# One single expert slot moved from behind eight double slots to in front of them

## The chip, the core and the metric

The kernel runs on one core of one Trainium2 chip. The time is that of the device for one execution, in microseconds (us); the median of three runs counts. The profile is of one further execution, which has a time of its own.

## What is computed

Three layers follow one another. The first is an attention over 4 batches, 8 heads and 576 positions, which keeps only scores within `tau` of the maximum. The second is a layer of eight experts. Each of the 2304 tokens goes to one of them:

```python
for s in range(S):
    fresh_e = int(np.argmax(logits[b, s]))
    e = fresh_e if s == 0 or local_gate[b, s] < 0.5 else (prev_e if prev_e >= 0 else fresh_e)
    prev_e = e
    ...
    h = np.maximum(x[b, s] @ w1[e], 0.0)      # w1[e]: 512 x 1024
    out[b, s] = p[e] * (h @ w2[e])            # w2[e]: 1024 x 512
```

The third mixes tokens and channels: `theta = x @ w_theta`, then `u = x + w_tok_r @ (x cos theta) + w_tok_i @ (x sin theta)`, and `u + relu(u @ w_ch)`. Everything is in float32.

## The kernel before

The experts work in **slots**. A single slot is 128 tokens of one expert, a double slot (a "two") is 256 tokens of one expert. Three early single slots are settled when three of the four batches are routed; they run first, in the order 2, 1, 0, while the last batch is being routed. Then come the late slots, found by `late_slots` from the final counts: eight twos (`NTWOS`), one single (`NSINGLE`), and two single slots called final (`NFINAL`), which hold no token of the first batch. In all there are 14 slots in `self.states`; below they go by their place, 0 to 13. Before, places 3 to 10 are the twos, 11 is the single and 12 and 13 are the finals.

`late_slots` writes a small table, `order_tab`, of three rows: where in the list of tokens a slot begins, its expert, and whether that expert differs from the one of the slot before. SyncE reads the table (`load_index` L911, `load_w1`). The third entry is the condition of the eight loads of 512 KB with which a slot gets its expert's weights, 4.19 MB: four of `w1` into `w1r` and three parts of `raw` (L961), four of `w2` into four `w2r` (L973). Where it is 0 the loads are issued and move nothing, and the slot uses what lies in the buffers.

A load is split into a high and a low part, by ScalarE and VectorE (`split`, L1096 and L1097); of `w1` and `w2` a single slot splits three quarters and a two splits all. The buffer `xt` for a slot's token rows has one copy. GpSimd gathers the rows into it (`gather`, L924) with the indices that SyncE has loaded (`load_index`, L916), and TensorE transposes them out of it (`tokens`, L938).

`slot_step` runs place `i`. It issues the gather of the next slot first. For a single slot (`single_step`) TensorE then does, in this order: `hidden` of this slot (L1023 to L1029), `tokens` of the next, `finish_slot` of the last if that was single (L1062 to L1066), `hidden_out` of this slot (L1049). SyncE's `load_index` for the slot after the next comes behind the load of this slot's fourth part of `w2`, and that waits until `finish_slot` of the last slot has read the buffer with L1066. For a two (`two_step`) TensorE does the four parts of `hidden_two` (L994 to L996), with `finish_slot` of the last slot among them if that was single, then `tokens` of the next, then `finish_two` (L1011 to L1013). Steps that decode the weights of the third layer (`decode`; GpSimd's share is L1168 and L1176) stand in the twos. Results go to DRAM by `scatter` (L1085) once ScalarE has scaled them (L1079).

TensorE, ScalarE and VectorE keep the order that is written out by hand in a step; the order on SyncE and GpSimd is a planner's. After place 13, all engines pass a branch on the number of left-over slots (L761), and the third layer begins with L1366.

Of the kernel before, what the change touches and what calls it, by code (L numbers as in the profile page):

```python
# [31 lines left out]
NEARLY, NTWOS, NSINGLE, NFINAL, MAXSINGLE = 3, 8, 1, 2, 8  # L32
# [20 lines left out]
class Kernel:  # L53
# [574 lines left out]
    def late_slots(self):  # L628

        nc = self.nc  # L630
        cnt = self.counts()
        yield
        used = self.early["used"]
        ni = self.small("late_ni", [1, E], I32)
        nc.vector.scalar_tensor_tensor(ni, used[:, :E], float(-P), cnt, ALU.mult, ALU.add)
        nc.vector.tensor_scalar(ni, ni, float(P - 1), None, ALU.add)
        nc.vector.tensor_scalar(ni, ni, 7, None, ALU.logical_shift_right)
        nf = self.small("late_nf", [1, E])
        nc.vector.tensor_copy(nf, ni)
        yield  # L640


        odd = self.small("late_odd", [1, E], I32)
        nc.vector.tensor_scalar(odd, ni, 1, None, ALU.bitwise_and)
        key = self.small("late_key", [1, E])
        nc.vector.scalar_tensor_tensor(key, odd, 16.0, self.slotj[:, 1:1 + E], ALU.mult, ALU.add)
        has = self.small("late_has", [1, E])
        nc.vector.tensor_tensor(has, nf, self.slots0, ALU.is_gt)
        nc.vector.tensor_tensor(key, key, has, ALU.mult)
        top = self.small("late_top", [1, 2])  # L650
        nc.vector.tensor_reduce(top[:, 0:1], key, AX.X, ALU.max)
        rest = self.small("late_rest", [1, E])
        nc.vector.scalar_tensor_tensor(rest, key, top[:, 0:1], key, ALU.is_lt, ALU.mult)
        nc.vector.tensor_reduce(top[:, 1:2], rest, AX.X, ALU.max)
        fin = self.small("late_fin", [1, E])
        nc.vector.scalar_tensor_tensor(fin, key, top[:, 1:2], has, ALU.is_ge, ALU.mult)
        nc.vector.tensor_tensor(nf, nf, fin, ALU.subtract)
        fbase = self.small("fin_base", [1, E + 1])
        nc.vector.memset(fbase, 0.0)
        nc.vector.tensor_tensor(fbase[:, :E], used[:, :E], nf, ALU.add)  # L660
        nc.vector.tensor_copy(ni, nf)
        final = yield from self.slot_table("final", NFINAL, 1, fin, fbase)
        yield
        nc.vector.tensor_scalar(ni, ni, 1, None, ALU.logical_shift_right)
        ntwo = self.small("late_two", [1, E])
        nc.vector.tensor_copy(ntwo, ni)
        twos = yield from self.slot_table("twos", NTWOS, 2, ntwo, used)
        yield
        two = twos["used"]
        nc.vector.scalar_tensor_tensor(nf, two[:, :E], -2.0, nf, ALU.mult, ALU.add)  # L670
        base = self.small("late_base", [1, E + 1])
        nc.vector.scalar_tensor_tensor(base, two, 2.0, used, ALU.mult, ALU.add)
        single = yield from self.slot_table("single", MAXSINGLE, 1, nf, base)

        yield
        n, m = NTWOS + NFINAL + MAXSINGLE, NTWOS + NSINGLE
        tab = self.small("order_tab", [1, 3, n])
        nc.vector.tensor_copy(tab[:, :2, :NTWOS], twos["tab"])
        nc.vector.tensor_copy(tab[:, :2, NTWOS:m], single["tab"][:, :, :NSINGLE])
        nc.vector.tensor_copy(tab[:, :2, m:m + NFINAL], final["tab"])  # L680
        nc.vector.tensor_copy(tab[:, :2, m + NFINAL:], single["tab"][:, :, NSINGLE:])
        e = tab[:, 1]
        nc.vector.tensor_tensor(tab[:, 2, 0:1], e[:, 0:1], self.early["tab"][:, 1, 0:1], ALU.not_equal)
        nc.vector.tensor_tensor(tab[:, 2, 1:], e[:, 1:], e[:, :n - 1], ALU.not_equal)
        tabi = self.cpool.tile([1, 3, n], I32, name="order_tabi")
        nc.vector.tensor_copy(tabi, tab)
        self.late = dict(tabi=tabi, total=single["total"])
# [45 lines left out]
    def first_loads(self):  # L733

        self.w1raw = [self.w1r] + [self.raw[:, i * F:(i + 1) * F] for i in range(3)]
        slots = [("early", j, False) for j in reversed(range(NEARLY))]
        slots += [("late", j, j < NTWOS) for j in range(NTWOS + NSINGLE + NFINAL)]
        self.states = [
            dict(slot=s[:2], two=s[2], first=i == 0, final=i >= len(slots) - NFINAL, extra=False) for i, s in enumerate(slots)]
        self.load_index(self.states[0])  # L740
        self.load_w1(self.states[0], 0)
        for st in self.states[1:NEARLY]:
            self.load_index(st)
# [825 lines left out]
```

## Time and profile before

| what | value |
|---|---|
| three runs | 858.43, 859.72 and 860.22 us, median 859.72 us |
| the profiled execution | 859.51 us, of which the profile's span is 857.8 us |
| TensorE busy | 814.5 us, 95% of the span |
| VectorE, ScalarE, GpSimd busy | 614.5, 494.2 and 211.9 us |
| read from and written to DRAM | 98.67 and 16.58 MB |

The attention takes about the first 303 us, the experts follow to 603.39 us, where the third layer begins. A row of the timeline has the start in us from the span's start, the duration in us, the engine, the line, the operation, what it writes and reads, and a count; a bracket gives the time for which the engine sat idle before it and what ended that. Matmuls overlap their neighbours, so a piece of work is measured from the start of its first instruction to the start of what follows.

### The profile page before, as it was taken

Reading aid. Unit: us, or ns where it says so; the run is one execution under the profiler, and the core shown is the slowest. Engines: PE = TensorE matmul, PEld = TensorE weight load, DVE = VectorE, ACT = ScalarE, POOL = GpSimd, SP = SyncE. Lnnn points to the kernel's source line nnn. Section 1 sums busy time; section 2 is a strip of 40 time slices with the busy share of each in tenths; the row PEclk is TensorE's granted clock in tenths of the full one; section 3 lists DMA queues with packets and bytes.
Section 4 is the critical chain, followed back from the end, with each engine's and each line's share of the span. In section 5 each row is a group of like instructions: output and inputs, shape, how many; then the busy total and the mean of one; then the engine's idle time right before and its main releaser. Section 6 shows DMA issues by size and latency. Waiting matters only on the chain. (4 is left out here: it accounts for less than half of the span.)

```text
span 857.8 us, 15181 instructions
## 1 busy us (share of the span) xinstructions
PE 814.5 (95%) x5554; PEld 655.2 (76%) x5554; DVE 614.5 (72%) x1281; ACT 494.2 (58%) x883; POOL 211.9 (25%) x209
## 2 busy tenths in 40 slices
PE   7999999999999898899999999989788999999997
PEld 4555655656566555789999899856778999999997
DVE  6888788888979849859888987544498845755432
ACT  5888777877777745656555555545654445535311
POOL 3000002002003014426555544101153520332120
PEclk9999999999999999999999999999898999999999
DMA  6622213322431369278777787666012030030101
GB/s 167 156 63 75 85 58 94 89 58 70 114 90 38 98 228 230 62 239 303 269 273 257 235 286 233 235 209 190 17 50 72 16 105 1 2 105 1 56 1 56
DMA packets 67241, 106.88 MB, mean 125 GB/s; under 512 B 28370, under 2 KB 34902, under 8 KB 67160
## 3 DMA queue, kind: packets, MB, share of 16 engines
q1 hardware_dynamic: 62968, 95.33, 36.3%
q0 software_dynamic: 4192, 10.51, 3.6%
q8 instruction: 46, 0.75, 0.4%
q14 instruction: 35, 0.29, 0.1%
HBM read 98.67 MB, written 16.58 MB: 134 GB/s over the span
## 5 line engine op out<-in xcount | busy, mean ns | idle before, releaser
L315 ACT ACTIVATE e<-ns,nb 128x576 f32<-128x576 f32 x144 | 112.1, 779 | 43.5 <-DVE ns L309 41.5
L309 DVE TENSOR_SCALAR_CACHE_REDUCE ns<-s,nqs 128x576 f32<-128x576 f32 x144 | 116.8, 812 | 25.4 <-PE s L289 14.3
L347 DVE SCALAR_TENSOR_TENSOR a<-ns,thr,e 128x576 f32<-128x576 f32 x144 | 117.2, 814 | 1.7 <-ACT thr L322 1.3
L289 PE MATMUL s<-raw 64*128 64x288 f32 x512 | 87.3, 440 | 7.7 <-DVE ns L309 7.1
L362 ACT ACTIVATE aT<-t 128x512 f32<-128x512 f32 x128 | 70.4, 594 | 21.7 <-PE t L361 20.8
L402 PE MATMUL o<-aT,vm 128*64 128x288 f32 x512 | 76.3, 418 | 0.0
L994 PE MATMUL h<-xh,stk 128*128 128x256 f32 x256 | 73.2, 286 | 0.0
L995 PE MATMUL h<-xl,stk 128*128 128x256 f32 x256 | 72.5, 283 | 0.0
L996 PE MATMUL h<-xh,stk 128*128 128x256 f32 x256 | 72.4, 283 | 0.0
L361 PE MATMUL t<-ident,a 128*128 128x128 f32 x512 | 69.6, 276 | 1.5 <-ACT aT L362 1.5
L1097 DVE TENSOR_TENSOR w2l<-w2r,w2h 128x1024 fp32r<-128x1024 f32 x50 | 64.8, 1311 | 7.5 <-ACT w2h L1096 7.4
L289 PEld LDWEIGHTS s<-raw 64*128 64x128 f32 x512 | 42.0, 185 | 36.1 <-DVE ns L309 17.0
L361 PEld LDWEIGHTS t<-ident,a 128*128 128x128 f32 x512 | 57.0, 141 | 14.2 <-issue 10.1
L402 PEld LDWEIGHTS o<-aT,vm 128*64 128x64 f32 x512 | 31.5, 136 | 37.0 <-issue 23.8
L1096 ACT ACTIVATE w2h<-w2r 128x1024 fp32r<-128x1024 f32 x50 | 52.2, 1061 | 10.4 <-DMA w2r<-in_moe_w_dram 7.9
L1011 PE MATMUL o<-w2h,hh 128*128 128x512 f32 x128 | 50.6, 395 | 0.0
L1012 PE MATMUL o<-w2l,hh 128*128 128x512 f32 x128 | 50.1, 391 | 0.4 <-DVE w2l L1097 0.4
L1013 PE MATMUL o<-w2h,hl 128*128 128x512 f32 x128 | 50.0, 390 | 0.0
L994 PEld LDWEIGHTS h<-xh,stk 128*128 128x128 f32 x256 | 49.1, 192 | 0.8 <-DVE hl L999 0.3
L995 PEld LDWEIGHTS h<-xl,stk 128*128 128x128 f32 x256 | 49.1, 192 | 0.5 <-issue 0.2
L996 PEld LDWEIGHTS h<-xh,stk 128*128 128x128 f32 x256 | 49.1, 192 | 0.0
L1097 DVE TENSOR_TENSOR stk<-raw,stk 128x1024 fp32r<-128x1024 f32 x36 | 43.9, 1241 | 7.2 <-ACT stk L1096 7.0
(382 smaller groups left out, 2160.0 us busy)
## 6 DMA issues: line engine op xcount, KB each, us to landing
w2r<-in_moe_w_dram SPq DMA_DIRECT2D x56, 512.0 KB
raw<-in_moe_w_dram SPq DMA_DIRECT2D x42, 512.0 KB
raw<-in_q_dram SPq DMA_DIRECT2D x15, 576.0 KB
w1r<-in_moe_w_dram SPq DMA_DIRECT2D x14, 512.0 KB
raw<-in_k_dram SPq DMA_DIRECT2D x30, 176.0 KB
vm<-in_v_dram SPq DMA_DIRECT2D x32, 128.0 KB
scr_x<-x SPq DMA_DIRECT2D x16, 256.0 KB
out_dram<-ob SPq DMA_DIRECT2D x16, 256.0 KB
```

Source lines behind the costliest of these rows:

```text
L289: nc.tensor.matmul(s[:, z, :SH], qd[rows, int(j != z), cs], kd[rows, j * KH:j * KH + SH], start=True, stop=True)
L309: nc.vector.tensor_scalar(ns, s[:, :, :SH], self.nqs[:, 0:1], None, ALU.mult, ALU.min, accum_out=nb)
L315: self.nc.scalar.activation(e, pr["s", c, j], AF.Exp, bias=pr["nb", c][:, j:j + 1], scale=-1.0)
L347: nc.vector.scalar_tensor_tensor(a.rearrange("p (z s) -> p z s", z=2), s, thr, e, ALU.is_le, ALU.mult, accum_out=total)
L361: nc.tensor.transpose(t[:, i, :], al(c)[:, k * P:(k + 1) * P], self.ident)
L362: nc.scalar.activation(aT[:, 4 * j:4 * j + 4, c * P:(c + 1) * P], t, AF.Copy)
L402: nc.tensor.matmul(o[j * D:(j + 1) * D, :SH], vm[:, j, c - 1, :], aT[:, 4 * j + c - 1, zs], start=(z == 0 and c == 1), stop=(z == 1 and c ...
L994: nc.tensor.matmul(h[:, i], wh[:, fs], xh, start=(k == 0), stop=False)
L995: nc.tensor.matmul(h[:, i], wh[:, fs], xl, start=False, stop=False)
L996: nc.tensor.matmul(h[:, i], wl[:, fs], xh, start=False, stop=(k == 3))
L1096: nc.scalar.activation(hi, raw, AF.Copy)
L1097: nc.vector.tensor_tensor(lo, raw, hi.bitcast(F32), ALU.subtract)
```

## The change

In `order_tab` and in the list of slots the single slot comes in front of the twos. It has place 3 now, the twos have 4 to 11, and the finals stay at 12 and 13. The two copies into `order_tab` write other columns; the row that tells whether the expert differs is worked out from the new order by the same instructions.

```diff
-        nc.vector.tensor_copy(tab[:, :2, :NTWOS], twos["tab"])
-        nc.vector.tensor_copy(tab[:, :2, NTWOS:m], single["tab"][:, :, :NSINGLE])
+        nc.vector.tensor_copy(tab[:, :2, NSINGLE:m], twos["tab"])
+        nc.vector.tensor_copy(tab[:, :2, :NSINGLE], single["tab"][:, :, :NSINGLE])
...
-        slots += [("late", j, j < NTWOS) for j in range(NTWOS + NSINGLE + NFINAL)]
+        slots += [("late", j, NSINGLE <= j < NTWOS + NSINGLE) for j in range(NTWOS + NSINGLE + NFINAL)]
```

## Rows read from the trace of the kernel before

**Rows 1.** Stretches: us, busy per engine (instructions), granted TensorE clock, DMA share, GB/s.

```profile
303.00:360.70 57.70, 51.07 (x243) 35.17 (x243) 46.16 (x137) 30.98 (x48) 20.77 (x14) 0.94 0.66 176
360.70:553.20 192.50, 192.13 (x1234) 174.46 (x1233) 149.20 (x165) 105.96 (x143) 87.41 (x56) 1.00 0.76 253
553.20:603.40 50.20, 42.10 (x166) 28.73 (x164) 21.91 (x24) 25.12 (x38) 5.99 (x6) 0.97 0.58 195
```

**Rows 2.** Timeline of TensorE, behind the twos, places 11 to 13.

```profile
553.21 0.39 PE L1023 MATMUL h<-stk,xh 128*128 128x512 f32 x1
...
559.00 0.60 PE L938 MATMUL t<-ident,xt 128*128 128x128 f32 x4
...
560.86 0.50 PE L1023 MATMUL h<-stk,xh 128*128 128x512 f32 x1 [0.82 <-ACT xh L941]
...
570.37 1.09 PE L938 MATMUL t<-ident,xt 128*128 128x128 f32 x4 [2.58 <-DMA xt<-scr_x,idx]
571.11 0.78 PE L1062 MATMUL o<-w2h,hh 128*128 128x512 f32 x1
...
578.13 0.60 PE L1049 MATMUL t<-ident,h 128*128 128x128 f32 x4
579.50 0.50 PE L1023 MATMUL h<-stk,xh 128*128 128x512 f32 x1 [0.77 <-ACT xh L941]
...
585.84 0.79 PE L1062 MATMUL o<-w2h,hh 128*128 128x512 f32 x1
...
592.08 1.04 PE L1049 MATMUL t<-ident,h 128*128 128x128 f32 x8
593.56 0.50 PE L1062 MATMUL o<-w2h,hh 128*128 128x512 f32 x1 [0.44 <-ACT hh L1050]
...
598.76 1.96 PE L1066 MATMUL o<-w2r,hf 128*128 128x512 f32 x4 [0.55 <-DMA w2r<-in_moe_w_dram]
603.39 0.74 PE L1366 MATMUL v<-ident,raw 128*128 128x128 f32 x5 [2.68 <-PEq L761]
```

**Rows 3.** Stretches, columns as in rows 1: ten us behind the longest stall.

```profile
570.00:580.00 10.00, 8.86 (x32) 6.39 (x32) 3.84 (x4) 4.97 (x8) 0.00 (x0) 0.83 0.62 228
```

**Rows 4.** Timelines of GpSimd, SyncE and ScalarE in the same stretch.

```profile
542.72 0.99 POOL L924 DMA_INDIRECT xt<-scr_x,idx  x1 [10.25 <-PE t L938]
...
563.74 1.43 POOL L924 DMA_INDIRECT xt<-scr_x,idx  x1 [8.39 <-PE h L1025]
...
563.21 2.64 SPq L973 DMA_DIRECT2D w2r<-in_moe_w_dram  x3
...
600.97 0.69 ACT L1079 ACTIVATE raw<-o,idx 128x512 f32<-128x512 f32 x1 [6.91 <-DMA scr_m<-raw,idx]
```

**Rows 5.** Timeline of TensorE ahead of the first two.

```profile
353.28 0.63 PE L938 MATMUL t<-ident,xt 128*128 128x128 f32 x4 [0.42 <-DMA xt<-scr_x,idx]
353.67 0.48 PE L1062 MATMUL o<-w2h,hh 128*128 128x512 f32 x1
...
359.71 1.04 PE L1049 MATMUL t<-ident,h 128*128 128x128 f32 x8
```

**Rows 6.** Stretches, columns as in rows 1, and SyncE's timeline ahead of the first two.

```profile
350.00:360.00 10.00, 9.57 (x42) 6.54 (x41) 8.62 (x11) 8.85 (x12) 1.48 (x2) 1.00 0.24 75
...
350.85 1.67 SPq L961 DMA_DIRECT2D raw<-in_moe_w_dram  x3
359.78 0.07 SPq L973 DMA_DIRECT2D w2r<-in_moe_w_dram  x1
360.38 0.38 SPq L916 DMA_DIRECT2D idx<-scr_list  x1
```

**Rows 7.** Timeline of GpSimd ahead of the first two.

```profile
341.79 5.42 POOL L1176 TENSOR_TENSOR th<-w 128x512 fp32r<-128x512 f32 x3 [10.30 <-DMA w2r<-in_moe_w_dram]
...
349.48 0.96 POOL L924 DMA_INDIRECT xt<-scr_x,idx  x1 [0.30 <-issue]
...
362.96 0.98 POOL L924 DMA_INDIRECT xt<-scr_x,idx  x1 [11.18 <-DMA idx<-scr_list]
```

## The prediction

> **What bounds the kernel now.** I read the stretches first. From 360.70 to 553.20 us, the eight twos, TensorE is busy for 192.13 of 192.50 us at the full granted clock [rows 1]: nothing but matmul work counts there, and 253 GB/s of transfers lie hidden beside it. In the stretches on either side, where single slots run, it is busy for 51.07 of 57.70 and 42.10 of 50.20 us, at granted 0.94 and 0.97. So the change is worth what it does to waits in these two stretches, since every matmul, split, gather and scatter is still made. Next I read TensorE's timeline there, for the bracketed waits [rows 2, 5], and then the queues that they name [rows 4, 6, 7].
>
> The end goes thus [rows 2]. Place 11 begins at 553.21, its hidden layer lasts until the transposes of place 12's tokens at 559.00, and place 12's hidden layer begins at 560.86 after a wait of 0.82. Then TensorE waits 2.58 for the gathered tokens of place 13 and transposes them at 570.37. That gather could only be issued at 563.74, since the one buffer was read at 559.00 by place 12, and three weight loads went out at about the same time, from 563.21 on [rows 4]. After the wait the clock falls: granted 0.83 in 570 to 580, a mix of 2.4 and 1.2 GHz [rows 3]. Further waits of 0.77, 0.44 and 0.55 follow, then the branch.
>
> **Which loads the change removes.** I worked the experts of the slots out of the reference's routing with its inputs. The final counts of the eight experts are 521, 178, 345, 351, 172, 172, 227 and 338. After three batches 354, 123, 254, 274, 138, 152, 182 and 251 are there, so the early slots have experts 0, 0 and 2 and run as 2, 0, 0. What is left is 3, 2, 2, 3, 2, 2, 2 and 3 slots; the finals take one of 3 and one of 7, the twos are of 0 to 7, the single is of 0. Before, the order is 2, 0, 0, then 0 to 7, 0, 3, 7; after, 2, 0, 0, 0, then 0 to 7, 3, 7. Twelve slots fetched weights, eleven will: 4.19 MB less. The trace bears out how a skipped load looks: three loads of 512 KB for place 3 are issued from 350.85 on, 1.57 MB in all, but the ten us from 350 to 360 moved only 75 GB/s, 0.75 MB in sum [rows 6]; the repeated 0 was skipped.
>
> Do the bytes themselves cost time? The end moved 195 GB/s and the twos 253 without a wait [rows 1], so the end was held by the order of its steps more than by the rate. I take nothing for bytes. The Trainium skill (DMA: Bandwidth & Descriptors, section Specifications) puts the limit from memory at about 358 GB/s for a core; by it 195 is no ceiling, and fewer bytes in the end gain nothing by themselves. Were 195 the ceiling, the 4.19 MB would be 21.5 us instead of the 19.2 below, and the sum 852.1.
>
> **The end, after.** With the single gone, two slots follow the last two. Place 12 now stands where 11 stood: its tokens were transposed within the last two, so the buffer is free early and the gather for 13 goes out as that at 542.72 did, some 16 us ahead of its use [rows 4]. The path of TensorE, from rows 2: hidden layer of 12, tokens of 13 and the wait of 0.82, which stays, 553.21 to 560.86, 7.65. Hidden layer of 13, 579.50 to 585.84, 6.34. Finish of 12, 585.84 to 592.08, 6.24. Transposes of 13 with the wait of 0.44, to 593.56, 1.48. Finish of 13 up to L1066, 5.20 less the wait of 0.55, since its last load has no third slot's weights ahead of it, 4.65. From L1066 to the third layer, 4.63. Sum 31.0 against 603.39 - 553.21 = 50.2: **19.2 us less**. What is late next is w2 of place 13: its loads go out at 563.21 as those of 12 did, and the finish needs it at about 575. ScalarE's wait of 6.91 for the scatter before the last scaling [rows 4] ends at 600.97, just behind TensorE; it may give back up to 0.6, which I leave out.
>
> **The head, after.** Place 3 is a single in front of the first two. It adds to TensorE one hidden layer, 559.00 - 553.21 = 5.79 [rows 2]; one finish, 359.71 - 353.67 = 6.04, and its transposes, 1.04 [rows 5]; and one set of token transposes, about 0.5. Sum 13.4. The wait of 0.42 for the second half of the first two's tokens [rows 5] goes, since place 3 has one half.
>
> The new wait is that of place 4's tokens. They need both halves, gathered into the one buffer after place 3's have left it, and the indices. SyncE loads these behind the fourth part of w2 for place 2, which waits for the finish of place 1: 359.78, then 360.38, and GpSimd could start at 362.96, 2.6 later [rows 6, 7]. Half a token set and the wait of 0.42 less, all that comes 0.9 earlier: the index load at 359.5, gathers from 362.0 to 363.0 and 363.3 to 364.3. From the end of its issue (349.48 + 0.96) to its use at 353.28 a gather took 2.8 in this quiet stretch [rows 5, 7], so the halves land at 365.9 and 367.1. TensorE wants them when the finish of 1 (358.7), the transposes (1.04) and the hidden layer (5.79) are done, at 365.5, and the second half 0.5 later: a wait of 1.1. Its bounds are 0 (a quicker landing) and, were it as slow as the gather at 563.74, done at 565.17 and used at 570.37, 5.2 instead of 2.8, about 3.5. I take 1.1, by the nearest row. Behind it stand finish, transposes and the first two. Splits of place 3 and 4 lie on ScalarE and VectorE, 8.85 and 8.62 us busy in the ten us to 360 [rows 6]; the work of a single is spread over 13.4 us of TensorE, so I cost it at nothing; without that cover each split of 1.2 would count whole. Head: 13.4 + 1.1 - 0.4 = **14.1 us more**.
>
> The twos move as a block and stay bound by TensorE; the other column numbers in the table cost nothing.
>
> **The sum.** -19.2 + 14.1 = -5.1 on the profiled execution's 859.51 us (span 857.8 and 1.7 around it), which lies 0.21 below the median: **854.4 us**. With the head's wait at 0 and the 0.6 of the scatter, 852.7; at 3.5, 856.8.
>
> **Rivals.** *The end keeps its gather wait.* If the planner puts the gather for 13 behind other work again, 2.58 stays and so does the slow clock behind it: the finish 571.11 to 578.13 took 7.02 against 6.24, and the transposes 0.3 more, together 1.1 [rows 2, 3]. 858.1. Against it: the buffer is free before the last two's second half.
>
> *GpSimd is late in the head.* Three squarings of decoded weights, 5.42, stood in front of place 3's gathers on its queue although the code has them later [rows 7]. In front of place 4's gathers they cost 5.4, and 1.1 for the clock: 860.9, no difference. Against it: they fit the 11.18 idle in front of 362.96.
>
> *The slower side: the index load falls behind the weight loads of place 4.* SyncE's order is the planner's. Place 4's fourth part of w1 may only be overwritten when place 3's hidden layer has read it, at 365.5. Indices loaded behind that go out at 366.1 instead of 359.5: 6.6 later, and 1.1 for the clock, 862.1. It is slower by over 0.2% once the gathers are about 5.8 later than I have them. Against it: 360.38 follows directly on 359.78 [rows 6].
>
> *The single isn't of expert 0.* Then places 3 and 4 both load; 4.19 MB at 253 GB/s [rows 1] are 16.6 us for a slot of 13.4, 3.2 more each, 860.8.
>
> **How the numbers follow.** Forecast 0.66, the wait at the end 0.12, GpSimd 0.10, indices 0.09, another expert 0.03. The range, 852.4 to 858.5, takes in the forecast's bounds and the first rival. A measurement here can tell about 0.2%, 1.7 us. The forecast is faster; the first rival lies on the border and counts as no difference, but for 0.02, as do GpSimd and most of the last; indices and the rest are slower: 0.68, 0.21, 0.11.
>
> **What would show it.** In the changed profile: the first two's L994 some 14 us later; a bracketed wait of about 1 us at L938 in front of it; no transfers for place 3; about 31 us from the last L1013 to L1366, without a wait for `xt`; full clock behind 553. A wait over 5 us at that L938, or slow clock behind it, would prove the sum wrong, as would waits of the twos.

## The result, and the profile after

The time fell from 860.03 us (median of 16 runs, 856.0 to 863.28) to 853.63 us (16 runs, 851.0 to 858.76). The ratio is 0.9917, its 95% interval 0.9902 to 0.9932: 7.1 us less, 5.8 to 8.4 (the ratio is taken over all runs; the two medians are 6.4 apart). The forecast was 854.4, that is 5.1 less, with a range of 852.4 to 858.5. The profiled execution of the kernel after took 853.75 us with a span of 851.8.

In the kernel after, every line from 678 on has a number one higher than before, so L938 is now L939, L1023 is L1024 and L1366 is L1367; an experiment that adds a line moves the numbers behind it once more. The stretches of the kernel after, with the columns of [rows 1]: the one ahead of the twos, the twos, the end.

```profile
303.00:376.95 73.95, 65.30 (x309) 44.66 (x303) 55.89 (x146) 41.95 (x63) 24.03 (x17) 0.95 0.54 149
376.95:568.89 191.94, 191.94 (x1234) 174.52 (x1233) 148.53 (x164) 105.98 (x143) 85.97 (x56) 1.00 0.74 252
568.89:598.55 29.66, 26.70 (x109) 18.32 (x108) 13.33 (x15) 16.05 (x24) 3.00 (x4) 1.00 0.53 182
```

The twos are as they were, bound by TensorE. The end shrank from 50.18 us [rows 2] to 29.66, by 20.5. The head grew. The head is counted here from the token transposes of place 3 to the transposes of the last single's hidden layer, which stand right ahead of the first two. In the kernel before it began with

```profile
352.26 0.60 PE L938 MATMUL t<-ident,xt 128*128 128x128 f32 x4
```

and ended at 359.71 [rows 5], 7.45 later; it is now 354.98 to 375.95, 20.97, so 13.5 more. Together -7.0, which is the measured change of 7.1. The two profiled spans themselves differ by 6.0: what lies ahead of the head was 2.7 longer in this execution (it differs by 2.2 among the profiles with the old order too), and the twos and the third layer were 1.7 shorter together.

TensorE's timeline in the end of the kernel after, from place 12 to the third layer:

```profile
568.89 0.39 PE L1024 MATMUL h<-stk,xh 128*128 128x512 f32 x1
...
574.69 0.60 PE L939 MATMUL t<-ident,xt 128*128 128x128 f32 x4
...
576.86 0.50 PE L1024 MATMUL h<-stk,xh 128*128 128x512 f32 x1 [1.14 <-ACT xh L942]
...
583.23 0.79 PE L1063 MATMUL o<-w2h,hh 128*128 128x512 f32 x1
...
589.47 1.04 PE L1050 MATMUL t<-ident,h 128*128 128x128 f32 x8
590.90 0.50 PE L1063 MATMUL o<-w2h,hh 128*128 128x512 f32 x1 [0.39 <-ACT hh L1051]
...
595.38 1.88 PE L1067 MATMUL o<-w2r,hf 128*128 128x512 f32 x4
598.55 0.74 PE L1367 MATMUL v<-ident,raw 128*128 128x128 f32 x5 [1.30 <-ACTq L762]
```

The path that the prediction laid out is walked step by step: 7.97, 6.37, 6.24, 1.43 and 4.48 us for what it had at 7.65, 6.34, 6.24, 1.48 and 4.65. Only the last step, from L1067 to the third layer, is far off: 3.17 for 4.63. No wait names `xt` here and the granted clock of the stretch is 1.00, against 0.97 in [rows 1].

TensorE's timeline in the head of the kernel after:

```profile
354.98 0.60 PE L939 MATMUL t<-ident,xt 128*128 128x128 f32 x4
...
368.24 0.63 PE L939 MATMUL t<-ident,xt 128*128 128x128 f32 x4
369.56 0.63 PE L939 MATMUL t<-ident,xt 128*128 128x128 f32 x4 [0.69 <-DMA xt<-scr_x,idx]
...
375.95 1.04 PE L1050 MATMUL t<-ident,h 128*128 128x128 f32 x8
```

And what stands in front of that wait, SyncE's and GpSimd's timelines:

```profile
362.07 0.38 SPq L917 DMA_DIRECT2D idx<-scr_list  x1
...
364.68 0.99 POOL L925 DMA_INDIRECT xt<-scr_x,idx  x1 [12.56 <-DMA idx<-scr_list]
365.97 0.96 POOL L925 DMA_INDIRECT xt<-scr_x,idx  x1 [0.30 <-issue]
```

The predicted new wait for place 4's tokens is there, at 0.69 us instead of 1.1. The gathers leave 2.6 us after the index load, as predicted.

Place 3's loads were skipped. A stretch of ten us of the kernel after, then SyncE's issue of its first load and ScalarE's split that uses it:

```profile
355.00:365.00 10.00, 10.00 (x48) 7.66 (x47) 7.36 (x8) 6.97 (x11) 0.32 (x1) 1.00 0.02 1
...
352.26 0.07 SPq L962 DMA_DIRECT2D w1r<-in_moe_w_dram  x1
...
352.42 1.06 ACT L1097 ACTIVATE stk<-w1r 128x1024 fp32r<-128x1024 f32 x1 [3.57 <-DMA w1r<-in_moe_w_dram]
```

1 GB/s moved while a single ran; the same ten us moved 150 and 154 GB/s in e4 and e3 (below), where place 3 loads. On the page of the kernel after, the hardware queue carried 91.13 MB against 95.33 before: 4.2 MB less, one slot's weights.

### The profile page after: what moved, and what is told of

It reads as the page before. It is cut to its first block, busy times and chain, and to the rows that moved or that the text cites. A ratio compares the mean times of both kernels' runs of the same rounds, so it can differ in the third digit from the quotient of the medians.

```text
span 851.8 us, 15179 instructions
## 1 busy us (share of the span) xinstructions
PE 810.8 (95%) x5554; PEld 652.0 (77%) x5554; DVE 615.5 (72%) x1281; ACT 494.3 (58%) x883; POOL 209.8 (25%) x209
## 3 DMA queue, kind: packets, MB, share of 16 engines
q1 hardware_dynamic: 61304, 91.13, 34.8%
```

## The experiments

Two theories were set against each other for the end, and one question was asked of the head. The prediction's theory: the end was held by the order of its steps, the gather for place 13 above all, and bytes cost nothing. The theory of the loads: the waits were for the weights of places 12 and 13, and the gather's wait only stood in front of a longer one. For the head: why does another single cost no more there than its own work?

The table gives each run's median, the median of the kernel before beside it, the ratio with its interval, and two spans of its profiled execution: the end (from the first hidden matmul behind the last two to the third layer) and the head as defined above (not listed where the single is not at place 3). One profile's span may stand 2 us off what the medians say; so it is in e1 and e5.

| run | median | before | ratio (95%) | end | head |
|---|---|---|---|---|---|
| before | 860.03 | | | 50.18 | 7.45 |
| after | 853.63 | 860.03 | 0.9917 (0.9902 to 0.9932) | 29.66 | 20.97 |
| e1 | 858.25 | 859.16 | 1.0002 (0.9986 to 1.0018) | 48.09 | |
| e2 | 859.79 | 859.16 | 1.0008 (0.9994 to 1.0021) | 49.35 | |
| e5 | 856.77 | 858.99 | 0.9975 (0.9961 to 0.9990) | 46.22 | |
| e6 | 850.43 | 858.99 | 0.9910 (0.9886 to 0.9934) | 42.25 | |
| e11 | 852.59 | 860.95 | 0.9897 (0.9870 to 0.9924) | 29.18 | |
| e3 | 858.14 | 859.16 | 1.0002 (0.9983 to 1.0021) | 29.85 | 27.12 |
| e4 | 858.47 | 859.16 | 0.9985 (0.9968 to 1.0003) | 30.00 | 26.58 |
| e7 | 860.20 | 858.99 | 1.0012 (0.9996 to 1.0027) | 31.49 | |
| e8 | 862.06 | 858.99 | 1.0036 (1.0014 to 1.0058) | 30.97 | |
| e9 | 850.41 | 860.95 | 0.9888 (0.9856 to 0.9919) | 30.71 | 19.84 |
| e10 | 852.98 | 860.95 | 0.9905 (0.9880 to 0.9931) | 29.19 | 20.99 |
| e12 | 852.85 | 860.95 | 0.9901 (0.9878 to 0.9924) | 29.33 | 19.84 |

### e1: the kernel before without the gather for place 13

```
 def gather(self, st, xt=None):
     if "xt" in st:
         return
+    if st is self.states[-1]:
+        st["xt"] = self.states[-2]["xt"]
+        return
```

> The kernel before, with the gather for place 13 left out: that slot uses the rows of place 12. Theory 1, by which the prediction priced the end: the wait of 2.58 us for these rows and the slow clock behind it (1.1) are costs of their own, so the time falls by 3 to 3.7 us, and place 13's hidden layer begins about 3.5 us earlier counted from the end of the twos than the 26.3 of before (553.21 to 579.50). Theory 2: the gather was covered by the weights; ScalarE waited for place 13's first w1 part until 573.11 and for the second until 576.09, so the hidden layer can't begin much earlier whatever TensorE did in between: 0 to 1 us.

TensorE's and ScalarE's timelines of e1, place 13 (lines behind the edit are three higher than before), and last ScalarE's row of the kernel before:

```profile
573.22 1.06 ACT L1099 ACTIVATE stk<-w1r 128x1024 fp32r<-128x1024 f32 x1 [8.28 <-DMA w1r<-in_moe_w_dram]
...
576.09 0.66 PE L1052 MATMUL t<-ident,h 128*128 128x128 f32 x4 [1.96 <-ACT h L1039]
577.91 0.79 PE L1026 MATMUL h<-stk,xh 128*128 128x512 f32 x1 [1.16 <-ACT xh L944]
...
573.11 1.06 ACT L1096 ACTIVATE stk<-w1r 128x1024 fp32r<-128x1024 f32 x1 [8.26 <-DMA w1r<-in_moe_w_dram]
```

The wait of 2.58 for `xt` is gone, and the hidden layer of place 13 begins 24.62 us behind the last two instead of 26.29: only 1.7 earlier. The rest came back as waits of 1.96 and 1.16 for ScalarE, which itself sat 8.28 waiting for the first part of w1, as it had sat 8.26 before. The time is the same. So the gather's wait was mostly cover for a load's; as a price of 2.58 plus a slow clock it was wrong.

### e2: the kernel before without the loads of place 11, the single

```
+nc.vector.memset(tab[:, 2, NTWOS:NTWOS + 1], 0.0)
```

The line stands behind the one that works out the load flags of the table; e3 to e6 and e11 have the same form.

> The kernel before with the loads of the single at place 11 left out (that slot uses the weights of expert 7): 4.19 MB less, order as before. If the bytes of the repeated expert are what the change saves: 3 to 6 us faster. If those loads lie beside the twos anyway and what counts is that two singles instead of three follow one another: within 1 us of before, with the wait for the rows of place 13 still there.

TensorE's and ScalarE's timelines of e2, behind place 12's hidden layer:

```profile
570.62 0.63 PE L939 MATMUL t<-ident,xt 128*128 128x128 f32 x4 [1.81 <-DMA xt<-scr_x,idx]
...
574.32 1.06 ACT L1097 ACTIVATE stk<-w1r 128x1024 fp32r<-128x1024 f32 x1 [8.43 <-DMA w1r<-in_moe_w_dram]
```

No gain: these bytes, the very ones that the change removes, cost nothing where they stood. They moved while the last twos ran. What ScalarE waits for is the load of the slots behind, 8.43 us, against 8.26 in the kernel before.

### e5 and e6: the kernel before without the loads of place 12, and of 12 and 13

```
+nc.vector.memset(tab[:, 2, m:m + 1], 0.0)
```

in e5, and in e6:

```
+nc.vector.memset(tab[:, 2, m:m + NFINAL], 0.0)
```

> The kernel before with the loads of place 12 left out (that slot uses the single's weights): 4.19 MB less between the twos and the last slot. In the two runs before, ScalarE waited 8.3 to 8.4 us for place 13's first w1 part, issued at about 567 behind the loads of w2 for place 12. If these loads are what stretches the end, place 13's part lands at once, and the 50.2 us from the twos to the third layer shrink by 3 to 4.5 us. If the order of the steps does it whatever is loaded: less than 1 us.

> The kernel before with the loads of places 12 and 13 both left out: three single slots follow the twos with no weights to wait for. By the theory that loads stretch the end: as e5 or up to 1.5 us better, some 45 to 46.5 us from the twos to the third layer, which is three slots of 13.4 us and the branch, and still far above the 29.7 of the changed kernel, since the third slot's own work stays. By the rival that it is the order: about 50.

ScalarE's split of place 13's first part of w1 in e5, then in e6:

```profile
571.95 1.06 ACT L1097 ACTIVATE stk<-w1r 128x1024 fp32r<-128x1024 f32 x1 [5.93 <-DMA w1r<-in_moe_w_dram]
```

```profile
567.00 1.06 ACT L1097 ACTIVATE stk<-w1r 128x1024 fp32r<-128x1024 f32 x1 [1.79 <-DMA w1r<-in_moe_w_dram]
```

The end falls to 46.22 and 42.25, by 4.0 and 7.9: more for e6 than was expected. It is the theory of the loads that holds. Where the loads stood is seen in the kernel before itself, in stretches of five us (columns of [rows 1]), on SyncE and on ScalarE:

```profile
565.00:570.00 5.00, 2.79 (x9) 1.31 (x7) 1.38 (x3) 0.00 (x0) 0.17 (x1) 1.00 0.99 336
570.00:575.00 5.00, 4.63 (x16) 3.90 (x17) 0.80 (x1) 1.06 (x1) 0.00 (x0) 0.66 1.03 413
...
566.78 0.35 SPq L961 DMA_DIRECT2D w1r<-in_moe_w_dram  x1
567.43 1.73 SPq L961 DMA_DIRECT2D raw<-in_moe_w_dram  x3
...
560.84 2.98 ACT L1096 ACTIVATE w2h<-w2r 128x1024 fp32r<-128x1024 f32 x3
```

Three loads of w2 for place 12 go out from 563.21 [rows 4] and four of w1 for place 13 right behind them: seven of 524,288 bytes, 3.67 MB, in six us. The DMA engines are then full, share 0.99 and 1.03 (as the profile counts it, it can come out above 1), and carry 336 and 413 GB/s, 3.7 MB in the ten us. The stretch's mean of 195 GB/s [rows 1], on which the prediction rested, hides that. They come together because place 11 is a single: its three splits of w2 run one upon the other on ScalarE, 2.98 us from 560.84, and only as they end does place 12's w2 go out, into the buffers that they read, with place 13's w1 behind it. Behind the last two the same loads are spread. SyncE's timeline of the kernel after:

```profile
554.79 8.96 SPq L974 DMA_DIRECT2D w2r<-in_moe_w_dram  x3
564.68 0.34 SPq L962 DMA_DIRECT2D w1r<-in_moe_w_dram  x1
```

Place 12's w2 is fetched over 8.96 us within the last two, and the first part of place 13's w1 is on its way 4.2 us before the last two ends at 568.89, with two of the other three behind it.

### e11: the kernel after without the loads of places 12 and 13

```
+nc.vector.memset(tab[:, 2, m:m + NFINAL], 0.0)
```

> The changed kernel with the loads of places 12 and 13 left out (both use the weights of the last two). On the kernel before, the same cut the end from 50.2 to 42.3 us. Theory: the end of the changed kernel has no wait for weights left, so 29.7 stays within 1.0. Rival: two singles still wait for loads, as the last one does for its w1: 26 to 28.

The end goes from 29.66 to 29.18. So 0.5 us is all that loads cost in the end of the kernel after, against 7.9 before. With it the 20.5 us split up: e6 less e11 is the single's own work, 42.25 - 29.18 = 13.07 us, and 7.93 - 0.48 = 7.45 are waits for loads, the step to the third layer behind them included. The single's own work costs about as much in either place, 13.1 us here and 13.5 in the head; what the change gains is these 7.45 us of waits.

### e4 and e3: the kernel after with weights fetched anew for place 3, and for 3 and 4

```
+nc.vector.memset(tab[:, 2, 0:1], 1.0)
```

in e4, and in e3:

```
+nc.vector.memset(tab[:, 2, 0:2], 1.0)
```

> The changed kernel, but place 3 loads expert 0 anew; place 4 keeps it. By the theory that the skip carries the head: about 8 us more than the changed kernel, 860 to 863, near or over the kernel before. By the rival that loads find room in the head: within 1 us of the changed kernel.

> The changed kernel, but places 3 and 4 both load expert 0 anew instead of keeping it. If the skip is what makes the head cheap: place 3 wants its first w1 part where it is issued, and 2.1 MB take about 8 us at 253 GB/s, so place 3 alone is some 8 us late, place 4 some 3 more; 862 to 868 us, slower than before. If the gain comes from the end alone and the loads find room in the head: within 2 us of the changed kernel, 853.6.

TensorE waiting for place 4's tokens and a stretch of five us in e4; then ScalarE's first split for place 4 and a stretch in e3:

```profile
372.66 0.63 PE L940 MATMUL t<-ident,xt 128*128 128x128 f32 x4 [3.76 <-DMA xt<-scr_x,idx]
...
365.00:370.00 5.00, 3.91 (x16) 2.38 (x14) 2.99 (x5) 3.07 (x7) 2.96 (x2) 1.00 0.91 326
```

```profile
373.81 1.06 ACT L1098 ACTIVATE stk<-w1r 128x1024 fp32r<-128x1024 f32 x1 [9.02 <-DMA w1r<-in_moe_w_dram]
...
370.00:375.00 5.00, 3.16 (x10) 2.71 (x11) 0.10 (x1) 1.06 (x1) 0.00 (x0) 0.53 1.02 412
```

The head grows by 5.6 and 6.2 us, to 26.58 and 27.12. By the ratios, 0.9985 and 1.0002 against 0.9917, 5.8 and 7.3 us are lost: less than expected, but nearly the whole gain in e4 and all of it in e3. It is the picture of the old end: loads bunched behind a single and DMA shares of 0.91 and 1.02. In e3 a split waits 9 us for its weights (8.3 in the old end). In e4 place 4 loads none, and it is its tokens that come late beside these loads: their wait is 3.76 instead of 0.69.

### e7 and e8: the single as second, and in the middle of the twos

```
-nc.vector.tensor_copy(tab[:, :2, :NTWOS], twos["tab"])
-nc.vector.tensor_copy(tab[:, :2, NTWOS:m], single["tab"][:, :, :NSINGLE])
+nc.vector.tensor_copy(tab[:, :2, :AT], twos["tab"][:, :, :AT])
+nc.vector.tensor_copy(tab[:, :2, AT:AT + 1], single["tab"][:, :, :NSINGLE])
+nc.vector.tensor_copy(tab[:, :2, AT + 1:m], twos["tab"][:, :, AT:])
...
-slots += [("late", j, j < NTWOS) for j in range(NTWOS + NSINGLE + NFINAL)]
+slots += [("late", j, j != AT and j < NTWOS + NSINGLE) for j in range(NTWOS + NSINGLE + NFINAL)]
```

AT is 1 in e7 and 4 in e8.

> The single directly behind the first two (place 4), which keeps expert 0 as the changed kernel does; eleven slots load. The next two's expert is loaded while the single runs. Theory: the end is that of the changed kernel, and the single has twos on either side, so it has no finish of a slot before it in its step, and indices come early; 2.1 MB of w1 at 253 GB/s take 8.3 us for a step of some 7.8, so 0 to 2 us more than the changed kernel, 853 to 856. Rival, by the e3 and e4 runs, where loading beside a single cost 5 us: 858.

> The single in the middle of the twos, behind that of expert 3 (place 7): it loads expert 0 again, twelve slots load as before. If what counts is only that the single leaves the end: 854 to 857, within 2 us of the single directly behind the first two. If the change gains through the 4.19 MB that it doesn't load: no faster than before, 858 to 861.

Both missed. ScalarE, TensorE and a stretch of five us around the slot behind the single, in e7 and in e8:

```profile
398.51 1.06 ACT L1098 ACTIVATE stk<-raw 128x1024 fp32r<-128x1024 f32 x1 [4.96 <-DMA raw<-in_moe_w_dram]
...
405.17 0.58 PE L996 MATMUL h<-xh,stk 128*128 128x256 f32 x1 [7.41 <-ACT xh L943]
...
395.00:400.00 5.00, 2.77 (x13) 1.50 (x11) 0.40 (x1) 1.06 (x1) 1.86 (x2) 1.00 1.00 372
```

```profile
469.49 1.06 ACT L1098 ACTIVATE stk<-raw 128x1024 fp32r<-128x1024 f32 x1 [5.50 <-DMA raw<-in_moe_w_dram]
...
474.74 0.58 PE L996 MATMUL h<-xh,stk 128*128 128x256 f32 x1 [7.65 <-ACT xh L943]
...
465.00:470.00 5.00, 2.09 (x11) 1.12 (x9) 0.25 (x1) 0.51 (x1) 2.29 (x2) 0.99 1.01 398
```

The end is as short as in the kernel after, give or take 2 us, but a new wait of 7.4 or 7.7 us stands behind the single, since the two that follows needs another expert's weights. In e7 the single's own weights need no load at all, and the wait is there all the same: it is the next slot's load that counts. The account closes roughly: for e7, the end's 31.49 - 50.18 = -18.7, the single's 13.1 and the wait's 7.4 make +1.8; measured +1.0 (0.0012 of 859). For e8 the same sum gives +1.5, against +3.1 measured (0.0036), so 1.6 us are not explained. Two loads of decode weights (512 and 576 KB in e7, twice 576 KB in e8) stood among the w1 loads; their share of the wait was not separated.

### e9, e10 and e12: the index load ahead, and the last two slots exchanged

```
+        if after and "idx" not in after:
+            self.load_index(after)
         if now:
             for c in range(4):
                 self.load_w2(now, c)
             for c in range(3):
                 self.split_w2(now, c)
-        if after and "idx" not in after:
-            self.load_index(after)
```

That is e9, an edit of the kernel after. e10 writes the two columns of its final table in the other order, and e12 does both:

```
-nc.vector.tensor_copy(tab[:, :2, m:m + NFINAL], final["tab"])
+nc.vector.tensor_copy(tab[:, :2, m:m + 1], final["tab"][:, :, 1:])
+nc.vector.tensor_copy(tab[:, :2, m + 1:m + NFINAL], final["tab"][:, :, :1])
```

> The changed kernel with one edit on SyncE: a single slot's load of the indices for the slot after the next stands ahead of its loads of w2. By the step of the prediction that the first two's tokens wait behind these indices, the wait of 0.69 us at L939 (L938 before) is gone and the gathers for place 4 go out right after place 3's tokens, some 8 us earlier; the time falls by 0.7 us at most, within what can't be told from the changed kernel. If the rows themselves were late, the wait stays.

> The changed kernel with the finals in the order of experts 7, 3, so that place 12 keeps the weights of the last two: ten slots load. By the theory that a skipped load counts only where a wait for it was left: place 12's loads lie beside the last two, place 13's are asked for as before, so the 29.7 us from the twos to the third layer stay within 1, and the time within 0.2% of the changed kernel. By the rival that each skipped 4.19 MB is worth about 4 us, as e5 showed on the kernel before: 849 to 850.

> Both edits, e9 and e10, on the changed kernel. If the parts are as stated there: no wait above 0.3 us at the first two's tokens, the end at 29 to 30 us, and a time of 0 to 1.2 us below the changed kernel, about 0.99 of the kernel before. More than 3 us below it would speak for the rival of e10.

SyncE, GpSimd and TensorE in the head of e9:

```profile
354.75 0.38 SPq L917 DMA_DIRECT2D idx<-scr_list  x1
...
357.33 1.24 POOL L925 DMA_INDIRECT xt<-scr_x,idx  x1 [4.62 <-DMA idx<-scr_list]
...
366.99 1.04 PE L939 MATMUL t<-ident,xt 128*128 128x128 f32 x8
```

The index load goes out 7.1 us behind place 3's token transposes in the kernel after (354.98 to 362.07) and 0.8 behind them in e9 (353.98 to 354.75), and the wait of 0.69 is gone: its cause, SyncE's order, is confirmed, and the head is 1.1 us shorter in e9 and in e12. e9 has the best ratio of all, but its interval overlaps that of the kernel after, and e12 has the same edit without a better time; that it beats the kernel after is not shown. The exchange of the last slots changes nothing that can be told, though it skips another slot's weights (86.94 MB on the hardware queue in e10, against 91.13).

## Why the prediction was right, and where it was not

**Sign and path: right.** Experts and skipped loads came as worked out (4.2 MB less, nothing moved for place 3), the end became two slots long by the steps named, the twos stayed bound by TensorE.

**The head: right, 0.6 too high.** 14.1 predicted, 13.5 measured. 0.4 of it is the wait for place 4's tokens, 0.69 for 1.1; that its cause was the index load behind a w2 load is shown by e9. The other rivals of the head didn't come: GpSimd's squarings were not in front of place 4's gathers, and the index load was not held by place 4's weights.

**The last term of the end: mis-sized.** The step was "From L1066 to the third layer, 4.63", taken over unchanged, with up to 0.6 for the scatter left out. It measured 3.17, 1.46 less, and that is the larger part of the 2 us by which the gain was too small. ScalarE and SyncE in the kernel after, then GpSimd and SyncE in the kernel before:

```profile
597.34 0.69 ACT L1080 ACTIVATE raw<-o,idx 128x512 f32<-128x512 f32 x1 [5.95 <-PE o L1067]
...
589.67 0.39 SPq L974 DMA_DIRECT2D w2r<-in_moe_w_dram  x1
```

```profile
597.70 0.98 POOL L1085 DMA_INDIRECT scr_m<-raw,idx  x1 [12.74 <-DMA raw<-scr_m]
...
590.05 2.35 SPq L1355 DMA_DIRECT2D raw<-scr_m  x5
...
592.76 0.41 SPq L973 DMA_DIRECT2D w2r<-in_moe_w_dram  x1
```

Two things held this step in the kernel before. One is the scatter that the prediction left out: the last scaling waited 6.91 for it [rows 4], and now waits only for TensorE's product. The other is TensorE's own pass of the branch, an instruction of its queue that lasts over 3 us. In the kernel before, then after (duration in ns, start in us):

```profile
L761 PEldq COMPARE_BRANCH  x1: 3389/3389/3389, 599.4 to 599.4; - x1
```

```profile
L762 PEldq COMPARE_BRANCH  x1: 3712/3712/3712, 594.2 to 594.2; - x1
```

Before, it began at 599.4, after the last products (L1066) had waited 0.55 for their weights, and ended at 602.8; the third layer, which TensorE's own queue held for 2.68 [rows 2], began at 603.39. After, it began 1.2 us ahead of these products and was over at 597.9; the third layer waited for ScalarE's pass of the branch instead. So the wait of 0.55, which the prediction took out of the step before, also stood in the 4.63 that it kept whole. In e1 the scatter is just as late (a wait of 12.66), but TensorE's branch begins in time, at 597.1: the step is 3.71 there, which puts the scatter at 0.5 of the 1.46 and the branch at 0.9. This split is read from rows; no run was made for it. By the rows both go back to the loads of place 13. ScalarE scaled place 11's results at 582.33, behind the splits that waited for these loads; five reads for the third layer (L1355) then waited 4.9 us on SyncE for the results to land; the scatter of place 12 waited for these reads, and the last part of w2 went out behind them, at 592.76. In e6, without these loads, the scaling comes at 574.45, the reads at 578.60, and the step is 3.03. In the kernel after place 11 is a two, and the reads are issued between 574.57 and 583.44.

**"I take nothing for bytes": wrong in its reason, harmless in the sum.** For the single's own 4.19 MB it held (e2). But the step said that "the end was held by the order of its steps more than by the rate", from a mean of 195 GB/s over 50 us. Inside it lay ten us at 336 and 413 GB/s with the DMA engines full, and 7.9 us of the end hung on loads (e6). The Trainium skill (DMA: Bandwidth & Descriptors, section Specifications), which the prediction weighed, puts the limit at about 358 GB/s; the five us at 413 lie above it, and the row decides. Order and rate work together here: the order bunches seven loads, and then the rate holds them. The sum didn't suffer, because TensorE's path in the changed end was laid out from rows without those waits. The prediction asked when the rows and the w2 of place 13 come, but not its w1, for which ScalarE had waited 8.26 us; that it came in time was not worked out, and there the prediction had luck. Had the loads stayed bunched, the same path would have been up to 7.45 us longer, by the split under e11, and that was a rival that the prediction did not have.

**The gather's wait, 2.58 and 1.1 for the clock: wrong as a price.** e1 took the gather away and gained nothing that can be measured, so in the old end this was no price; what such a wait would cost in the new end, as in the first rival, no run shows. Nor was it the buffer alone that held this gather, as the prediction has it: its indices were asked for only at 560.06, and in e5 and e6 the profile names them as what this gather waited for last.

**"Spread over 13.4 us of TensorE, so I cost it at nothing": right for a condition not named.** In front of the twos and among them, a single was seen to cost only its work where neither it nor the slot behind it needs new weights. Places 2, 3 and 4 are all of expert 0. e4 and e3 take that away, for place 3 and for both 3 and 4, and lose 5.8 and 7.3 us; in e7 and e8 the slot behind the single needs new weights, and TensorE waits 7.4 and 7.7. It is no law for every single: the two behind the last two load their weights and cost 0.5 us for it (e11).

**What is open.** Whether earlier loads in the old end, without moving the single, would have brought the same 7 us was not tried. How the step to the third layer shares out between the scatter and the branch has no run of its own.

## What to carry to other kernels

A short slot bunches the loads of the slots behind it; put it where neither it nor the next slot needs new weights, and count that before counting the bytes that it saves itself. Before pricing a named wait, look for the one that stands behind it on another engine: here a wait of 2.58 for a gather covered one of 8.3 for weights. Read the rate and the DMA share in stretches as short as the wait, not over the whole stage.

## What was not expected of the hardware

A skipped load costs its place in the queue 0.07 us, and its consumer started 0.16 us after the issue (352.26 and 352.42 above).

TensorE's pass of the branch ahead of the third layer took 3.35 to 3.83 us in all fourteen profiles, ScalarE's 0.05. In the kernel after the last products covered it, in the kernel before they did not (above).

The same wait before the same line left different clocks. Stretches of ten us of the kernel after and of e9, each with one wait of 3.0 us:

```profile
345.00:355.00 10.00, 7.50 (x25) 5.40 (x26) 8.65 (x9) 5.36 (x9) 6.41 (x4) 0.83 0.31 95
```

```profile
345.00:355.00 10.00, 6.97 (x32) 5.14 (x32) 8.65 (x9) 5.46 (x9) 7.25 (x4) 1.00 0.37 106
```

Granted 0.83 in one, a mix of 2.4 and 1.2 GHz, and 1.00 in the other: a price for the clock behind a wait of this length, as the prediction's 1.1, holds in some executions and not in others. And executions of one and the same kernel spread over 7.3 us (before, 856.0 to 863.28), more than most terms of the sum.
